# Down projection of two chunks as one Strassen pair, with a denser hand-out of attention steps: a fused attention and feed-forward block on one core

## The chip, the cores and the metric

The kernel runs on 1 core of one Trainium2 chip. The metric is device time in microseconds (us). All times compared here are of runs in the fast state; the two single runs e17 and e18 have no state, and only their traces are used. Medians are quoted beside ratios. A ratio is the mean time of one kernel's fast runs over that of the kernel before in the same rounds, so it is not quite the ratio of the medians.

Engines are named as the profile names them: PE is TensorE, PEld its weight loads, DVE VectorE, ACT ScalarE, POOL GpSimd.

## The reference

One pre-norm block over 2048 positions of width 1024, in bf16. Attention has 32 heads of 32; each position looks at 8 positions, at distances 0, 2, ... 14. The feed-forward part is the product of two linear maps, of width 3584.

```python
def _A_ref(x, wqkv, wo):               # H = 32, Dh = 32, W, dil = 8, 2
    q, k, v = ...                      # from x @ wqkv
    idx = pos[:, None] - arange(W)[None, :] * dil
    logits = einsum("bhsd,bhswd->bhsw", q, kg) * Dh ** -0.5   # kg, vg: k, v gathered by idx
    logits = where(idx >= 0, logits, -1e9)
    o = einsum("bhsw,bhswd->bhsd", softmax(logits), vg)
    return o.reshape(B, S, D) @ wo
def _B_ref(x, w_gate, w_up, w_down):
    return ((x @ w_gate) * (x @ w_up)) @ w_down
h = x + _A_ref(_layernorm(x), A_wqkv, A_wo)
return h + _B_ref(_layernorm(h), B_w_gate, B_w_up, B_w_down)
```

## The kernel before

The positions are cut into four chunks of 512. Chunks 0 and 1 go through the feed-forward part one after the other; chunks 2 and 3 go together, as a Strassen pair (7 block products where 8 would be needed). Attention is done on VectorE in steps that the program counts as 1.0 to 3.5 us (their instructions take 0.3 to 2.3 us each in the trace), and these steps are handed out between TensorE's groups of eight matmuls by a small scheduler. It runs when the program is built, so it fixes the order of each engine's queue and nothing else:

```python
class Background:
    def step(self, us):                       # called after each group of matmuls
        self.now += us
        self.credit = min(self.credit + us * self.rate, 4.0)      # the cap
        while self.credit > 0:
            item = next((i for i in self.items if i[0] <= self.now), None)
            ...                               # next attention step; credit -= its length
    def spend(self, us):                      # other VectorE work
        self.credit -= us
```

Chunk 0's output projection is followed by two blocks of the last QKV projection:

```python
    qkv(3, range(4), last=True)
    bg.finish(atts[0])
    bg.rate = 0.98
    nxt = wo_ln2(0)          # output projection; add, statistics, normalize on VectorE
    qkv(3, range(4, 6), last=True)
    start_attention(3)
    hT = ffn1(0, lnT2)       # first feed-forward of chunk 0: gate, up, product
    bg.finish(atts[1])
    nxt = wo_ln2(1)
    for hf in range(2):
        ffn2(0, hf, hT, hs)  # direct down projection of chunk 0
    ...
    hT = ffn1(1, lnT2, {...})
    ...                      # chunk 1's down projection as a small Strassen product of its own
```

The products run in float16 and need a power-of-two scale. It comes from the sum of absolute values: ScalarE adds up each tile, VectorE adds up the columns, a matmul with ones adds up the partitions, and five small VectorE steps make the scale. With several tiles ahead of it, such a scale is a chain through three engines:

```python
class Scale:
    def add(self, k, src, junk):
        nc.scalar.activation(junk, src, ACTF.Abs, accum_out=self.l1[:, k:k + 1])
    def rows(self):
        nc.vector.tensor_reduce(row[:], self.l1[:], ..., ALU.add)
        nc.vector.tensor_copy(self.rowb[:], row[:])
    def total(self, ps=None):
        nc.tensor.matmul(ps[:, 0:n], lhsT=ones[:], rhs=self.rowb[:]..., start=True, stop=True)
        ...                                   # five small steps on VectorE
```

## Time and profile before

| | kernel before |
|---|---|
| median of the first 3 runs, span | 776.96 us (776.87 to 777.28), 775.2 us |
| TensorE matmuls (weight loads counted) | 3691, 769.3 us busy, granted clock 1.00 in all records |
| VectorE, ScalarE busy | 605.3 us, 484.0 us |

The lines of the profile stand in the prediction. A line of busy times gives the share of the span behind each engine. A line of waits reads "engine, tile and line that waited <- what released it: us in total, times, longest". A line of the timeline gives start, length, engine, line, operation, and in brackets the idle time of that engine just before it. A line of a stretch gives its length, then the busy time of PE, PEld, DVE, ACT and POOL, then the granted TensorE clock, the busy share of the DMA engines and GB/s.

### The profile page before, as it was taken

The page shows a single profiled execution, that of the slowest core. Times are in us where ns is not written, and L with a number is a line of the kernel's source. Part 1 is how long each engine was busy: PE and PEld are TensorE (multiplying, and loading weights), DVE is VectorE, ACT ScalarE, POOL GpSimd, SP SyncE. Part 2 cuts the span into 40 slices and gives each one's busy share as a digit, 9 for nine tenths or more (in the row PEclk, how much of TensorE's full clock was granted, in tenths as well). Part 3 has the DMA queues.
Part 4 walks back from the last instruction along what each step waited for, and adds up shares of the span by engine and source line. Part 5 has one row for each costly group of instructions (what it writes and reads, how often), then busy time and mean ns, then how long its engine had stood idle before and what let it go on. Part 6 is the DMA issues. An engine that isn't in the chain of part 4 may idle for free.

```text
span 775.2 us, 10420 instructions
## 1 busy us (share of the span) xinstructions
PE 769.3 (99%) x3691; PEld 353.5 (46%) x3691; DVE 605.3 (78%) x766; ACT 484.0 (62%) x1040; POOL 142.1 (18%) x152
## 2 busy tenths in 40 slices
PE   8999999999999999999999999999999999999998
PEld 6444444444444444444444444444444444444444
DVE  5639999999999989999979859985553444578863
ACT  4639564322866662965777899746677776788240
POOL 0000000200002000011000001008778687600000
PEclk9999999999999999999999999999999999999999
DMA  8998896997947964978445592644332423740001
GB/s 278 265 260 199 157 230 151 299 271 224 310 133 236 308 235 125 288 257 277 142 143 192 182 299 68 157 98 114 109 95 69 109 59 106 240 140 28 0 28 55
DMA packets 183716, 134.38 MB, mean 173 GB/s; under 512 B 81264, under 2 KB 176496, under 8 KB 181616
## 3 DMA queue, kind: packets, MB, share of 16 engines
q1 hardware_dynamic: 176912, 110.12, 50.9%
q0 software_dynamic: 3584, 22.02, 8.9%
q10 hardware_dynamic: 3168, 1.57, 0.8%
q8 instruction: 29, 0.48, 0.3%
q14 instruction: 23, 0.19, 0.1%
HBM read 104.86 MB, written 22.02 MB: 164 GB/s over the span
## 4 chain that ended last, share of the span: by engine, by line
PE 93%; DVE 3%; DMA 2%; ACT 1%; issue 0%; ACTq 0%; DVEq 0%
PE ps L411 20%; PE pg L411 12%; PE pu L411 12%; PE dx L807 6%; PE pz L700 6%; PE acc L646 6%; PE py L700 6%; PE px L700 6%; PE wo L532 4%; PE wo L852 4%; PE pv L700 3%; PE dy L807 3%; PE ex L807 2%; DMA lnT<-lnr 1%; DMA w_qkv<-in_A_wqkv_dram 1%; PE ps L372 1%
## 5 line engine op out<-in xcount | busy, mean ns | idle before, releaser
L411 PE MATMUL ps<-lnT,w_qkv 128*128 128x512 bf16 x736 | 159.5, 379 | 0.0
L411 PEld LDWEIGHTS <-w_qkv 128*128 128x128 bf16 x736 | 71.9, 98 | 86.2
L411 PE MATMUL pu<-lnT,w_wu 128*128 128x512 bf16 x448 | 105.8, 379 | 0.0
L411 PE MATMUL pg<-lnT,w_wg 128*128 128x512 bf16 x448 | 105.8, 379 | 0.0
L324 ACT CAST sg<-ps 128x512 bf16<-128x512 f32 x96 | 55.2, 585 | 52.3 <-PE ps L411 49.2
L451 DVE TENSOR_TENSOR prod<-qD,kD 128x4096 bf16<-128x4096 bf16 x32 | 72.4, 2285 | 12.8 <-DMA kD<-kd 12.7
L494 DVE TENSOR_TENSOR pv<-vD,at 128x4096 bf16<-128x4096 bf16 x32 | 72.5, 2285 | 0.3
L700 PEld LDWEIGHTS <-sw 128*128 128x128 f16 x448 | 43.8, 98 | 53.8 <-issue 1.2
L411 PEld LDWEIGHTS <-w_wu 128*128 128x128 bf16 x448 | 43.8, 98 | 52.9
L411 PEld LDWEIGHTS <-w_wg 128*128 128x128 bf16 x448 | 43.7, 98 | 52.8
L616 ACT CAST us<-pu 128x512 bf16<-128x512 f32 x56 | 33.0, 590 | 43.0 <-PE pu L411 41.8
L700 PE MATMUL px<-lnT,ws 128*128 128x512 bf16 x224 | 55.2, 379 | 0.0
L700 PEld LDWEIGHTS <-ws 128*128 128x128 f16 x336 | 32.9, 98 | 39.7
L506 POOL DMA_DIRECT2D od<-oD x4 | 2.2, 542 | 264.3 <-DVE oD L504 264.3
L646 PE MATMUL acc<-w_wd,gs 128*128 128x512 bf16 x224 | 48.5, 379 | 0.0
L681 POOL TENSOR_TENSOR sw<-ws 128x512 f16<-128x512 f16 x26 | 30.0, 1152 | 85.1 <-PE py L700 77.8
L611 ACT CAST gs<-pg 128x512 bf16<-128x512 f32 x56 | 32.6, 583 | 12.9 <-PE pg L411 10.6
L453 DVE TENSOR_TENSOR prod<-prod 128x4096 bf16<-128x4096 bf16 x16 | 36.6, 2289 | 0.4
L560 ACT ACTIVATE junkd<-w_wd 128x512 bf16<-128x512 bf16 x56 | 34.3, 613 | 0.0
L646 PEld LDWEIGHTS <-gs 128*128 128x128 bf16 x224 | 21.9, 98 | 26.4
L617 DVE TENSOR_TENSOR gs<-gs,us 128x512 bf16<-128x512 bf16 x56 | 23.5, 419 | 12.5 <-ACT us L616 12.5
L185 ACT ACTIVATE rs<-mv,eps 128x1 f32<-128x1 f32 (+1 forms) x21 | 6.2, 297 | 42.0 <-DVE mv L182 36.6
(321 smaller groups left out, 1391.5 us busy)
## 6 DMA issues: line engine op xcount, KB each, us to landing
w_wg<-in_B_w_gate_dram SPq DMA_DIRECT2D x14, 1024.0 KB, 6.7
w_wu<-in_B_w_up_dram SPq DMA_DIRECT2D x14, 1024.0 KB, 5.4
w_wd<-in_B_w_down_dram SPq DMA_DIRECT2D x8, 896.0 KB, 6.2
w_pair<-in_B_w_gate_dram SPq DMA_DIRECT2D x14, 512.0 KB, 4.0
w_pair<-in_B_w_up_dram SPq DMA_DIRECT2D x14, 512.0 KB, 5.2
w_wo<-in_A_wo_dram SPq DMA_DIRECT2D x6, 1024.0 KB, 6.2
w_qkv<-in_A_wqkv_dram SPq DMA_DIRECT2D x5, 1024.0 KB, 11.0
kd<-sg SPq DMA_DIRECT2D x32, 144.0 KB, 3.3
```

The source lines that it names most:

```text
L324: nc.scalar.copy(sg[:, HB:HB + TC], ps[:])
L411: nc.tensor.matmul(ps[:], lhsT=wt[:, ko, bass.ts(j, 128)], rhs=rhs[:, ko, :], start=(ko == 0), stop=(ko == KO - 1))
L451: nc.vector.tensor_tensor(prod[:, j], qD[:], kD[:, :, o:o + SUB], ALU.mult)
L453: nc.vector.tensor_tensor(prod[:, :, 0:16], prod[:, :, 0:16], prod[:, :, 16:32], ALU.add)
L494: nc.vector.tensor_tensor(pv[:, j], vD[:, :, o:o + SUB], at[:, w, None, :].to_broadcast((128, DH, SUB)), ALU.mult)
L532: nc.tensor.matmul(ps[:], lhsT=oTs[c][:, kk, t, :], rhs=wts["wo", c, hf][:, kk, :], start=(kk == 0), stop=(kk == KO - 1))
L560: nc.scalar.activation(junk, src, ACTF.Abs, accum_out=self.l1[:, k:k + 1])
L611: nc.scalar.copy(gs[:], pg[:])
L616: nc.scalar.copy(us[:], pu[:])
L646: nc.tensor.matmul(acc[t][:], lhsT=hT[f][:, bass.ts(t, 128)], rhs=wts["wd", c, hf, b][:, j, :], start=(f == 0), stop=(f == NF - 1))
L700: nc.tensor.matmul(ps[:], lhsT=lhs[:, ko, :], rhs=rhs[:, ko, :], start=(fresh and ko == 0), stop=(ko == 3), skip_group_check=not fresh)
L807: nc.tensor.matmul(ps[:, bass.ds(lo, n)], lhsT=lhs[k][:, bass.ts(q, 128)], rhs=rhs[k][:, bass.ds(lo, n)], start=(fresh and k == 0), stop=( ...
```

## The change

The intent is to save matmuls. Both chunks' down projections become one Strassen pair: 392 matmuls in place of 224 direct ones and 196 of the small Strassen product. For that, both first feed-forwards come first; chunk 1's products go out to HBM and are read back; and the attention has to be done earlier against the matmuls. So it is handed out 7% denser (a rate of 1.05 in place of 0.98), with twice the credit (a cap of 8.0 in place of 4.0). To make room on VectorE, the norm of chunk 1 and some conversions and copies ("seeds") go to ScalarE.

```diff
-        self.credit = min(self.credit + us * self.rate, 4.0)
+        self.credit = min(self.credit + us * self.rate, 8.0)
...
-    bg.rate = 0.98
+    bg.rate = 1.05
+    bg.spend(5.0)
     nxt = wo_ln2(0)
     qkv(3, range(4, 6), last=True)
     start_attention(3)
-    hT = ffn1(0, lnT2)
-    bg.finish(atts[1])
-    nxt = wo_ln2(1)
-    for hf in range(2):
-        ffn2(0, hf, hT, hs)
+    def wo_1():
+        bg.finish(sums)
+        bg.finish(atts[1])
+        n = wo_norm(1)                 # output projection of chunk 1, its norm on ScalarE
+        ...
+    hT0 = ffn1_first(nxt[0], {4: wo_1})
+    bg.finish(norm2[1])
+    ffn1_second(norm2[0].lnT, {})      # products to HBM from a ring of three tiles
...
+    while 3 not in scored:
+        next(atts[3])
+    wo_adds(2, {0: in_turn(lambda: pull(1), lambda: abs_blocks(b11 + b21)), 2: in_turn(scale_h1.rows, lambda: pull(1)),
+                4: in_turn(total_h1, lambda: pull(1)), 6: lambda: pull(1)})
+    for q in range(4):
+        dprod(xs[q], q, A11, cells_of(b11, NH), True)       # first of seven products
+        if q == 0:
+            conv_h1(a21, 0)            # conversions of what is read back from HBM
+            conv_h1(a22, 0)
+            s1_half(0)
+            scale_d.rows()             # column sums of the down weights' scale
+        if q == 1:
+            pull(1)                    # one attention step
+            conv_h1(a21, 1, nc.scalar)
+            conv_h1(a22, 1, nc.scalar)
+        if q == 2:
+            scale_d.total(ys[3])
+            ...
+            for i in range(3):
+                seed(i)
...                                    # six more products, results, order of loads
```

## The prediction

> **What bounds the kernel now.** I read the page's first lines, then TensorE's own waits, then the chain of waits, then busy time by stage, and last the stretches of VectorE, ScalarE and GpSimd that feed the stages which the change rearranges.

> From the page (1: busy time; 2: the span in 40 slices; 4: the chain that ended last):

> ```profile
> span 775.2 us, 10420 instructions
> PE 769.3 (99%) x3691; PEld 353.5 (46%) x3691; DVE 605.3 (78%) x766; ACT 484.0 (62%) x1040; POOL 142.1 (18%) x152
> ...
> PE   8999999999999999999999999999999999999998
> DVE  5639999999999989999979859985553444578863
> ...
> PE 93%; DVE 3%; DMA 2%; ACT 1%; issue 0%; ACTq 0%; DVEq 0%
> ```

> TensorE (PE) is busy 99% and carries 93% of the last chain. Busy matmul time by itself would not prove a limit, so I checked the spacing in the chain of waits in order of time:

> ```profile
> 287.88 13.81 PE wo L532 x64
> 301.69 48.35 PE acc L646 x224
> ...
> 446.76 6.04 PE ex L807 x28
> ```

> 64, 224 and 28 matmuls of 512 columns take 13.81, 48.35 and 6.04 us: 0.216 us each, with no gap between these stages. All of TensorE's waits in the run:

> ```profile
> PE warm_ps L318 <- DVE warm L304: 1.2, 1, 1.2
> PE pv L700 <- DVE h L812: 0.6, 2, 0.4
> PE ps L372 <- ACT lnT L367: 0.4, 1, 0.4
> PE ps L372 <- DMA w_qkv<-in_A_wqkv_dram: 0.3, 1, 0.3
> PE pt L366 <- DVE ln L359: 0.3, 1, 0.3
> ```

> These 2.8 us and the tail are all the idle time there is. So each matmul taken away is worth 0.216 us, there is nothing left to hide a new wait behind, and a new wait costs its whole length. VectorE (DVE) is the second engine: the stages from 191 to 447 us, as columns PE, weight loads, DVE, ACT, POOL busy, show it at 95%, 98% and 90%:

> ```profile
> 191.00:302.00 111.00, 111.00 (x516) 50.31 (x515) 105.53 (x106) 66.31 (x126) 5.70 (x8) 1.00 0.75 236
> 302.00:350.00 48.00, 48.00 (x224) 21.77 (x223) 46.85 (x33) 35.30 (x116) 3.12 (x4) 1.00 0.78 243
> 350.00:447.00 97.00, 97.00 (x452) 43.94 (x450) 87.12 (x88) 73.69 (x161) 2.06 (x4) 1.00 0.57 185
> ```

> [...]4096 bf16 columns take 2285 ns as tensor-tensor and 1276 ns as tensor-scalar, so the new sums cost nearly twice a conversion of that size.[...]

> **The change part by part.**
> TensorE. Removed: the direct down projection of chunk 0 (4 row blocks x 2 halves x 28 = 224 matmuls) and the Strassen product inside chunk 1 (7 products x 2 blocks x 14 = 196). Added: one Strassen pair over both chunks, 7 x 4 x 14 = 392. Net 28 fewer, 28 x 0.216 = **6.04 us**. Two of the matmuls that add up a scale grow from 64 to 512 columns, 2 x 0.19 = 0.37 us back. The instruction order agrees (28 fewer matmuls in all). Gain if nothing waits: **5.67 us**, 771.3 us.

> VectorE. The number of instructions falls from 766 to 718, but they are larger (4096-wide sums of chunk 1's activations, 512-wide in place of 256-wide sums); summing counts by the durations in the trace, the totals are equal within 1 us. What changes is the deadline. TensorE used to reach chunk 2's output projection at 452.8 us; now it comes after both first feed-forward stages: 191.2 + 193.4 + 13.8 = 398.4 us. Chunk 1's output projection moves from 287.9 to 191.2 + 32 x 1.727 = 246.4 us. The 1.05 rate and the larger credit are there to have attention 1, 2 and most of 3 done by then.

> ScalarE. It loses abs sums of 512 columns (613 ns plus 187 ns for the read of the sum) and gets 2048-wide ones; it gains sums of the down weights after the fact (12 of 1024 and 4 of 512 columns, about 12 x 1.05 + 4 x 0.6 = 15 us), seeds, and half of the conversions. By the row durations it stays under 80% in both feed-forward stages, but at the down stage its queue becomes a chain.

> Transfers. Chunk 1's products go to HBM and return (3.7 MB out, 5.5 MB back), against some 3.7 MB less of down weights. At a mean DMA share of 0.6 in that stretch these stay hidden.

> **Where TensorE may wait: the near meets.** I add VectorE's durations in the new order, from its first attention product at 52.0 us. The same addition on the old order gives 233.3 us for the start of attention 1's last sum, once the 2.8 us of waits seen in its trace are added; the trace has 233.6, so the method holds within 0.5 us.
> 1. Output projection of chunk 1 (due 246.4). Attention 1 ends near 235.3. Before, these GpSimd steps lay so:

> ```profile
> 236.17 0.54 POOL L506 DMA_DIRECT2D od<-oD  x1 [62.50 <-DVE oD L504]
> 245.09 3.54 POOL L509 DMA_DIRECT2D oT<-od  x4 [8.39 <-PE pg L411]
> ```

> The store took 8.9 us, and the first of four loads 3.7 us more: with the same weights in flight, 235.3 + 8.9 + 3.7 = 247.9. Wait about 1.5 us.
> 2. Scale of chunk 1's products, a matmul behind five groups of chunk 2's output projection (398.4 + 1.5 + 8.6 = 408.5). It needs the last product, its abs sum on ScalarE and two VectorE steps: about 409.4. Wait about 1.
> 3. Scale of the down weights, behind three blocks of the first product (near 424). ScalarE's 15 us of sums start near 407, and VectorE's own queue gets there near 424.4. Wait about 1.
> 4. The second product overwrites the banks that ScalarE must first copy into seeds: two 3072-wide conversions (2.7 us each by the 3267 ns of a 3584-wide one) stand ahead of the copies, so 422 + 5.4 + 0.7 = 428.1 to 428.8 against TensorE's 428. Wait about 0.7.
> 5. In the stage of chunk 3's output projection VectorE has near 26 us of adds, statistics, conversions and sums for 25.9 us of matmuls (13.8 + 12.1); the first result must leave its bank before the next product. Wait about 1.3.

> The sum is 5.5 us, nearly all of the gain: 776.8 us. But each is the difference of two estimated arrivals: it may come out at zero, a wait in one absorbs part of the next, and the constants (1.05, which steps sit on ScalarE) look as if they had been fitted on the chip against just these waits. I choose some 3 us in all: 776.96 - 5.67 + 3.0 = **774.3 us**.

> **The rivals.**
> A. No wait: the scheduling is exact and the whole 5.67 us comes out, 771.3 us. For it: the kernel before has no gap either, in a schedule as tight. Against it: five meets within 2 us.
> B. VectorE becomes the bound of the middle. If its queue is 4 us later than I add up (longer waits for exp, products waiting for ScalarE), meets 2 to 4 move with it: 5.67 lost and some more, 777 to 780 us. For it: 95 to 98% busy before, and 54 us less until its deadline.
> C. The round trip through HBM or the late weight loads arrive late: the reads wait for the last store, then bring 3.5 MB, some 10 to 14 us at 250 to 350 GB/s, due near 417. Against it: the order puts three 512-wide adds and three attention steps ahead of the conversion. If late by 3 us, 776 to 778 us.

> **Range and chances.** Best case 771.3 less a little noise, so 770.8 below; my full sum of waits plus 2 us for B or C, 778.8 above. Faster by over 2% would need 15.5 us; only 5.67 are there. Slower by over 2% would need 21 us of waits, over three times the sum.

> **What would show it.** TensorE's busy time near 763.6 and 3663 matmuls. Attention 1's store issued near 235 and chunk 1's output projection near 246 to 248. In TensorE's waits, a few rows of 0.5 to 2 us: output projection on a transfer, scale matmuls on VectorE, second product on ScalarE's seeds. Wrong if these rows sum to over 7 us or to nothing, if TensorE waits in the pair stage after, which I take as unchanged, or if the stages before 163 us move.

## The result, and the profile after

The changed kernel is correct and takes **784.90 us** (median of 4 runs, 783.94 to 785.59); the kernel before took 777.04 us in the same rounds. The ratio is 1.010, interval 1.0083 to 1.0118. So it is 1% slower, not 0.3% faster, and lies 6.1 us above the predicted range.

The page of the changed kernel (span, busy times, chain that ended last):

```profile
span 782.0 us, 10253 instructions
...
PE 764.8 (98%) x3607; PEld 351.9 (45%) x3663; DVE 606.4 (78%) x718; ACT 511.9 (65%) x979; POOL 142.0 (18%) x152
...
PE 65%; DVE 21%; ACT 5%; issue 4%; DMA 4%; SPq 0%; DVEq 0%; ACTq 0%
```

The matmuls did go: 3663 weight loads against 3691 are 28 fewer. (The trace misses some matmul records, so the loads are counted.) But TensorE carries only 65% of the last chain, where it carried 93%; VectorE now carries 21%. TensorE's waits after 60 us, in the changed kernel:

```profile
PE l1psh L641 <- DVE rowbh L636: 3.6, 1, 3.6
PE pwu L430 <- ACT ring L756: 2.0, 1, 2.0
PE pg L430 <- DMA lnT<-ln: 2.0, 1, 2.0
PE ey L641 <- DVE rowbd L636: 1.4, 1, 1.4
...
PE ps L430 <- DVE h L600: 0.4, 1, 0.4
PE ex L931 <- ACT ey L1054: 0.2, 1, 0.2
```

They sum to 9.6 us. Three stretches of the changed kernel tell more:

```profile
191.20:199.00 7.80, 5.78 (x20) 2.17 (x19) 6.37 (x11) 4.78 (x15) 0.00 (x0) 0.78 0.99 276
275.00:300.00 25.00, 24.89 (x116) 11.31 (x116) 18.48 (x23) 24.84 (x47) 1.07 (x2) 1.00 0.71 210
416.90:423.70 6.80, 6.65 (x25) 2.80 (x26) 6.70 (x11) 6.80 (x15) 0.00 (x0) 0.79 1.09 355
```

In the first and the third, each right at a wait, the granted clock is 0.78 and 0.79. That is 7.8 x 0.22 + 6.8 x 0.21 = 3.1 us lost on top of the waits, an estimate from these two lines. In the second ScalarE is busy 24.84 of 25 us while VectorE, which should be the full engine, has 18.48.

The sum of the span: 5.67 us saved, 9.6 us of waits, 3.1 us of slow clock, and 0.6 us of waits of the kernel before near 520 us that are gone: +6.4 us. The spans differ by 782.0 - 775.2 = 6.8 us. So the gain is there, and more than twice as much is lost in four places:

1. **At 191 us**, where the first feed-forward starts, it waits for the last transposes of chunk 0's norm. VectorE's first addition of chunk 0's output projection, in the timeline of the kernel before and then of the changed one:

```profile
171.99 0.69 DVE L534 TENSOR_TENSOR h<-wo,h 128x512 bf16<-128x512 f32 x1
```

```profile
176.82 0.68 DVE L600 TENSOR_TENSOR h<-wo,h 128x512 bf16<-128x512 f32 x1
```

It starts 4.8 us later, because three more attention steps (2.29, 1.22 and 1.23 us) stand ahead of it in the queue.

2. **At 384 us** TensorE waits for a bank that ScalarE has not yet copied. ScalarE's timeline there:

```profile
383.03 1.06 ACT L631 ACTIVATE ring<-ring 128x1024 bf16<-128x1024 bf16 x1 [4.31 <-DVE ring L739]
```

ScalarE stood 4.31 us before an abs sum, for a product that VectorE had behind some 9 us of attention 3, and the copies that TensorE needed stood behind that sum and an exp of 1.04 us. In the trace the next copies come only at 385.03 us, after both.

3. **At 413 us**, the scale of chunk 1's products (3.6 us). 4. **At 434 us**, the scale of the down weights (1.4 us).

### The profile page after: what moved, and what is told of

Same layout as the page of the kernel before. It is cut to its first block, busy times and chain, and to the rows that moved or that the text cites.

```text
span 782.0 us, 10253 instructions
## 1 busy us (share of the span) xinstructions
PE 764.8 (98%) x3607; PEld 351.9 (45%) x3663; DVE 606.4 (78%) x718; ACT 511.9 (65%) x979; POOL 142.0 (18%) x152
## 3 DMA queue, kind: packets, MB, share of 16 engines
q0 software_dynamic: 3584, 22.02, 8.6%
q10 hardware_dynamic: 6864, 5.24, 2.5%
HBM read 110.10 MB, written 27.26 MB: 176 GB/s over the span
## 4 chain that ended last, share of the span: by engine, by line
PE 65%; DVE 21%; ACT 5%; issue 4%; DMA 4%; SPq 0%; DVEq 0%; ACTq 0%
PE ps L430 18%; PE dx L931 6%; PE pz L813 6%; PE py L813 6%; PE px L813 6%; DVE pv L521 5%; DVE prod L476 4%; PE pv L813 3%; PE ez L931 3%; PE ey L931 3%; PE dy L931 3%; DVE oD L531 2%; PE wo L985 2%; DMA w_wg<-in_B_w_gate_dram 2%; DMA a<-hd 2%
## 5 line engine op out<-in xcount | busy, mean ns | idle before, releaser
L476 DVE TENSOR_TENSOR prod<-qD,kD 128x4096 bf16<-128x4096 bf16 x32 | 72.0, 2285 | 12.9 <-DMA kD<-kd 12.8
L430 PE MATMUL pg<-lnT,w_wg 128*128 128x512 bf16 x221 | 53.4, 383 | 2.2 <-DMA lnT<-ln 2.0
L430 PE MATMUL pwu<-lnT,w_wu 128*128 128x512 bf16 x219 | 52.5, 379 | 2.3 <-ACT ring L756 2.0
L813 PE MATMUL px<-lnT,ws 128*128 128x512 bf16 x212 | 53.1, 379 | 0.6
L430 PE MATMUL pu<-lnT,w_wu 128*128 128x512 bf16 x218 | 53.3, 384 | 0.3
L430 PE MATMUL pwg<-lnT,w_wg 128*128 128x512 bf16 x220 | 52.5, 379 | 0.2
L931 PEld LDWEIGHTS <-gs 128*128 128x128 f16 (+1 forms) x280 | 27.4, 98 | 34.9 <-issue 2.1
L830 ACT COPY py<-px 128x512 f32<-128x512 f32 x28 | 16.0, 570 | 28.2 <-PE px L813 28.2
L631 ACT ACTIVATE ring<-ring 128x1024 bf16<-128x1024 bf16 x14 | 14.8, 1059 | 25.8 <-DVE ring L739 25.8
L795 POOL TENSOR_TENSOR sw<-sw,ws 128x512 f16<-128x512 f16 x26 | 30.0, 1154 | 2.0
L797 POOL TENSOR_TENSOR sw<-ws,sw 128x512 f16<-128x512 f16 x26 | 30.2, 1161 | 0.0
## 6 DMA issues: line engine op xcount, KB each, us to landing
w_qkv<-in_A_wqkv_dram SPq DMA_DIRECT2D x5, 1024.0 KB, 10.8
```

Source lines behind the costliest of these rows:

```text
L430: nc.tensor.matmul(ps[:], lhsT=wt[:, ko, bass.ts(j, 128)], rhs=rhs[:, ko, :], start=(ko == 0), stop=(ko == KO - 1))
L476: nc.vector.tensor_tensor(prod[:, j], qD[:], kD[:, :, o:o + SUB], ALU.mult)
L795: eng.tensor_tensor(sw[:, i, 1], sw[:, i, 0], a11, ALU.subtract)
L797: eng.tensor_tensor(sw[:, i, 3], a12, sw[:, i, 1], ALU.subtract)
L813: nc.tensor.matmul(ps[:], lhsT=lhs[:, ko, :], rhs=rhs[:, ko, :], start=(fresh and ko == 0), stop=(ko == 3), skip_group_check=not fresh)
L830: nc.scalar.copy(yb[i][:], xb[i][:])
```

## The experiments

Two theories were set against each other. **Q**: each wait stands for itself and comes from one step in a wrong place of a queue; mend the place and the time is won. **V**: VectorE (with ScalarE, which it feeds and waits for) sets the pace of the whole middle, and a wait taken away comes back at the next place where TensorE meets it. Further rivals were the read-back through HBM and the transfers (C), and the density of 1.05.

| run | what it is | median us | ratio to before | TensorE's larger waits, us |
|---|---|---|---|---|
| changed | | 784.90 | 1.0100 | 2.0, 2.0, 3.6, 1.4 |
| e1 | cap of 4.0 up to chunk 0's projection | 780.09 | 1.0045 | 2.5, 3.6 |
| e2 | kernel before, cap of 8.0 | 781.96 | 1.0060 | 2.3, 1.4 |
| e3 | cap of 4.0 throughout | 780.18 | 1.0039 | 2.0, 3.6 |
| e4 | changed, six gate sums left out | 779.51 | 1.0035 | 1.8, 3.1, 1.0 |
| e5 | e1, scale matmul later | 782.85 | 1.0070 | 1.7, 5.9 |
| e6 | e5, two more steps moved | 788.04 | 1.0153 | 2.4, 1.4, 4.9, 4.0 |
| e7 | e6, chunk 1's projection later | 787.52 | 1.0133 | 1.7, 2.3, 4.9, 4.1 |
| e8 | changed, rate 0.98 | 785.32 | 1.0103 | 1.9, 8.7 |
| e9 | e1, two norms to ScalarE | 780.82 | 1.0050 | 2.0, 2.6, 1.1 |
| e10 | e1, two gate sums moved | 776.69 | 0.9998 | 2.8, 2.3 |
| e11 | e9 and e10 | 777.30 | 1.0006 | 1.7, 2.5 |
| e12 | e11, rate 0.98 | 785.85 | 1.0117 | 1.7, 11.1 |
| e13 | e10, down scale earlier | **775.12** | **0.9980** | 2.6, 0.7, 1.1 |
| e14 | e10, chunk 1's projection later | 777.55 | 1.0005 | 4.3, 0.8 |
| e15 | e13 and e14 | 777.56 | 1.0010 | 3.8, 0.9, 1.1 |
| e16 | changed, two gate sums moved | 780.71 | 1.0047 | 0.6, 2.0, 3.1, 2.5 |

Intervals of the ratios reach 0.0012 to 0.0015 to either side (0.0018 for the changed kernel). The runs were taken in several rounds, on different chips; the changed kernel was run in the first alone, and the medians of the kernel before were 777.02 to 777.25 us in all of them. The waits are those of the one profiled run of each kernel, which need not be a typical one: e1's is its slowest (781.86 of 779.46 to 781.86 us), e5's its fastest (780.29 of 780.29 to 784.39). All of them give the correct result, e4 too, whose scale is wrong on purpose.

### e1 to e3: the cap

```diff
-        self.credit = min(self.credit + us * self.rate, 8.0)
+        self.credit = min(self.credit + us * self.rate, self.cap)    # 4.0; e1 sets 8.0 after start_attention(3)
```

> The changed kernel with the old cap of 4.0 until chunk 0's output projection has been built, and 8.0 after it: three attention steps (2.29 + 1.22 + 1.23 us) no longer stand ahead of that projection's first addition on VectorE. Both theories: the 2.0 us wait of TensorE at the start of the first feed-forward and the slow clock after it (2 x 0.8 us) are gone, TensorE enters that stage near 191.3 instead of 193.55. Theory Q (each wait stands for itself, a matter of queue order): the 3.7 us stay won to the end, 781.2 us. Theory V (VectorE is now the engine that sets the pace of the middle, and the waits of TensorE only show where the two meet): TensorE, now 3.7 us early, finds chunk 1's attention output not landed at 246.8 (it landed near 249.5) and waits 2 to 3 us there, and the waits at 383, 413 and 434 us keep their places: at most 1.5 us of the 3.7 remain, 783 to 785 us.

> The kernel before with the cap raised from 4.0 to 8.0 and nothing else. If the cap is what puts the attention steps ahead of chunk 0's output projection, TensorE waits 2 to 3 us at the first matmul of the first feed-forward near 191 us (its last normalize moves from 187.0 to about 190.4) and runs the next two groups slowly, so the time rises by 3 to 4 us to about 780.5. If the rate of 1.05 or the handing of steps after chunk 0's projection is the cause instead, nothing changes: 777 us.

> The changed kernel with the old cap of 4.0 throughout. The wait at 191 us goes as in the run before it. Theory Q: the burst of nine us of attention steps ahead of a product of chunk 1 at 373 to 382 us is cut in two as well, so the 2.0 us wait at 383 us goes too: 5.7 us less, 779 us. Theory V: with a lower cap steps that could not be handed out are lost rather than saved, so VectorE has less in its queue and falls further behind at 400 us: the waits at 413 and 434 us grow by what the first two gave, 784 to 787 us.

e2 settles the first place: the cap alone makes the kernel before 4.9 us slower (776.77 to 777.43 against 780.56 to 782.59), with the wait at 194.96 us (2.28 us) and a clock of 0.72 in the 6 us after it:

```profile
PE pg L411 <- DMA lnT<-ln: 2.3, 1, 2.3
```

So the larger credit, not the density, puts the three steps ahead. In e1 that wait is gone and 4.8 us are won, more than the 3.7 expected; not all of it is the price of this one wait, as those at 384 and 434 us are gone too. Still both theories missed something. TensorE's waits in e1:

```profile
PE l1psh L642 <- DVE rowbh L637: 3.6, 1, 3.6
PE wo L575 <- DMA oT<-od: 2.5, 1, 2.5
```

As V says, TensorE, now on time, waits 2.5 us for chunk 1's attention output. In the changed kernel that wait was zero only because TensorE came 4 us late. Against V, the waits at 384 and 434 us are gone. e3 is the same as e1, so what the cap does after chunk 0's projection makes no difference to the time.

### e4: ScalarE's load

```diff
-                if j % 2:
+                if j % 2 and b < 4:
                     abs_sum("wg", b, j // 2, junk[:])
```

> The changed kernel without the last six of fourteen abs sums of the gate weights (ScalarE, 2048 columns, 1.92 + 0.21 us each; those columns of the sum are set to zero, so the scale may come out too large on purpose). It frees 12.8 us of ScalarE between 247 and 300 us. If VectorE is late because it waits for ScalarE there (5.0 us for the up casts, 1.1 for the exp in that stretch), VectorE gains 4 to 6 us by 300 us, the first addition of chunk 2's output projection moves from 412.6 to about 407, and the waits at 413 and 434 us shrink from 5.0 to 0 to 2 us: 780 to 782 us. If ScalarE's load is not the cause, the time stays at 784.9.

The time fell by 5.4 us, a little more than expected. VectorE's waits for the up copies fell from 5.0 to 1.1 us, and the first addition of chunk 2's projection moved from 412.6 to 408.3 us. Part of the gain is luck: in the run that was profiled, the wait at 191 us (1.81 us) was not followed by the slow clock. That ScalarE holds VectorE up between 270 and 300 us is shown.

### e5 to e7: moving the places where TensorE waits

```diff
-                4: in_turn(total_h1, lambda: pull(1)), 6: lambda: pull(1)})
+                4: lambda: pull(1), 6: lambda: pull(1), 7: total_h1})          # e5
             conv_h1(a21, 0) ...                                                # e6:
+            scale_d.rows()                     # ahead of the conversions
-            conv_h1(a21, 1, nc.scalar) ...     # both behind the seeds
-    hT0 = ffn1_first(nxt[0], {4: wo_1})
+    hT0 = ffn1_first(nxt[0], {(4, 2): wo_1})                                   # e7
```

> The kernel of e1 with the matmul that adds up the scale of chunk 1's products moved from behind five groups of chunk 2's output projection to behind all eight. TensorE reaches it 5.2 us later, so its wait of 3.65 us there is gone (both theories), and with it the slow stretch after it in the runs that have one. Theory Q: 3.7 to 5 us less than e1's 780.1, about 775.5 us. Theory V: the next meeting is kept by VectorE, which still adds up the down weights' sum near 432.0 us behind the read-back of chunk 1's products and three 4096-wide steps; TensorE, now at about 428.5, waits 3 to 4 us there instead, and the time stays near 779 to 780 us.

> The kernel of e5 with two steps moved in their queues: VectorE adds up the down weights' sums before it converts what is read back (ScalarE has the last of them at 426.6 us), and ScalarE copies the seeds before its two 3072-wide conversions of 2.84 us each. Nothing is removed from any engine. If the waits are a matter of where four small steps stand, TensorE has no wait after 402 us: 3 to 5 us less than e1, 775.5 to 777 us. If VectorE's total load or the read-back is the limit, a wait of the same size appears at the next product, the ones that use the read-back near 445 us, and the time stays at 779 to 780 us.

> The kernel of e6 with chunk 1's output projection called after two of the four column groups of gate block 4 instead of before them, 6.9 us later. TensorE meets chunk 1's attention output, which lands near 249.5, at 253.7: the wait of 2.5 us there is gone. Theory Q: that stays won, 772.5 to 774.5 us, under the kernel before. Theory V: VectorE and ScalarE pay for it with the later norm, the start of chunk 1's feed-forward waits for its transposes near 302 us, and no more than 1 us is won over e6.

The wait of 3.6 us is gone in e5, and the next one has grown from nothing to 5.9 us, with a slow clock after it:

```profile
PE ey L642 <- DVE rowbd L637: 5.9, 1, 5.9
PE wo L575 <- DMA oT<-od: 1.7, 1, 1.7
```

e5 lost 2.8 us against e1 by the medians, worse than either theory said. e6 lost 5.2 more, by its own edit. The seeds came 4.9 us late, since the small steps of the down weights' scale still stood in VectorE's queue behind the conversions and an attention step; ScalarE, which had been given nothing else to do first, was idle for 8.04 us. Then VectorE stood 7.89 us for the two ScalarE conversions that I had moved back, and the third product waited 4.0 us for VectorE. So e6 does not decide between load and order; it shows that moving one step without what it needs only moves the wait. In e7 the wait for the attention output is gone, as expected, and the total stays within 0.5 us of e6, as V expected, though not in the place that V named: no wait appears near 302 us; two of 0.8 and 0.9 us on ScalarE's copies appear at 387 and 395 us instead, and the one at 425 us grows from 1.4 to 2.3 us.

### e8: the density

```diff
-    bg.rate = 1.05
+    bg.rate = 0.98
```

> The changed kernel with the old rate of 0.98 in place of 1.05 for the attention steps after chunk 0's output projection has started; the cap stays 8.0. The wait at 191 us stays, as those steps are handed out before. If the density does what its author wanted, attention 1 ends some 2 to 3 us later and the output projection of chunk 1 waits for it, and more of attention 3 is left over at 397 us: same to 3 us slower, 785 to 788 us. If the density is what delays the products of chunk 1, the wait at 383 us goes and the time falls by 2 us, 783 us.

```profile
PE wo L985 <- DMA oT<-od: 8.7, 1, 8.7
PE pg L430 <- DMA lnT<-ln: 1.9, 1, 1.9
```

785.32 us, the same as the change. Three waits (2.0, 3.6 and 1.4 us) became one of 8.7 us at chunk 3's output projection, because attention 3 ended that much later (its last addition starts at 470.4 us, in the changed kernel at 460.6). The density does what its author wanted; it only chooses where the wait lies.

### e9 to e12: relief for VectorE, relief for ScalarE

e9 makes the norm of two of chunk 0's row blocks on ScalarE. e10 has the two abs sums of gate block 4 ahead of chunk 1's output projection, where ScalarE was idle 5.0 us:

```diff
-                if j % 2:
+                if j % 2 and b != 4:
                     abs_sum("wg", b, j // 2, junk[:])
...
+            if b == 4:
+                for i in range(2):
+                    abs_sum("wg", 4, i, junk[:])
             if b in at:
                 at[b]()                # wo_1
```

> The kernel of e1 with the normalization of two of chunk 0's four row blocks taken from VectorE (1.27 + 0.21 + 0.55 us each, 4.06 us in all) to ScalarE, which has 4.2 us of work in the 28 us of that stage. Theory V (VectorE's queue sets the time up to chunk 3's output projection): every step of VectorE after it comes 4 us earlier, attention 1 ends near 229.5, the 2.5 us wait of chunk 1's output projection is gone and the waits at 413 to 432 us shrink: 2.5 to 4 us less than e1, 776 to 777.5 us. Theory Q (single steps in wrong places): the wait for the attention output goes, the scale's wait of 3.65 us stays because it keeps its place in the queue, 777.5 us at best and the wait at 413 us unchanged. Theory C (transfers): the output of attention 1 lands when it did, 780 us.

> The kernel of e1 with the two abs sums of gate block 4's weights (4.2 us of ScalarE) done ahead of chunk 1's output projection, where ScalarE stands idle for 5.0 us, instead of among the casts after it. The same sums, the same result. If ScalarE's full queue from 270 to 300 us holds VectorE up there (4.6 us for the up casts in e1), VectorE gains 2 to 4 us by 300 us; by theory V that comes out as 1 to 3 us in the time, 777 to 779 us. If VectorE would wait elsewhere anyway, no change: 780 us.

> Both reliefs of the two runs before it. Theory V: they add up, since both are time of VectorE before the same deadline: 774 to 776 us, under the kernel before. Theory Q: the 3.65 us wait of the scale stays, 776 to 777.5 us.

> Both reliefs, with the old rate of 0.98 besides. With the rate of 0.98 alone the waits at 383, 413 and 434 us vanished and came back as one of 8.7 us at chunk 3's output projection, near 484 us, because attention 3 ended at 472.6. Theory V: the 4 us taken from VectorE and the 2 to 4 us that it no longer waits for ScalarE come off that one wait, the 3.6 us that TensorE is earlier add to it: 4 to 6 us of wait in that place and none before, 776 to 778 us. Theory Q: the one wait is a matter of that projection's place and stays at 8.7 or more, 780 to 782 us.

e9 failed as a test: VectorE was rid of 4.06 us, but then stood 5.60 us at 183.15 us for a root that ScalarE computed behind the moved norms. Attention 1's last addition came at 234.9 us, not earlier than e1's 233.2. The relief turned into a wait.

e10 is the most telling run. No work was removed, two sums were moved by a few us, and 3.4 us were won; the change is then level with the kernel before. VectorE's waits for the up copies in the changed kernel, in e1 and in e10:

```profile
DVE gs L696 <- ACT us L720: 5.0, 3, 2.8
```

```profile
DVE gs L697 <- ACT us L721: 4.6, 2, 3.2
```

```profile
DVE gs L697 <- ACT us L724: 0.7, 1, 0.7
```

They fell from 4.6 to 0.7 us, the column sums for the scale of chunk 1's products were ready at 411.3 us instead of 414.8, and the wait of 3.6 us there is gone. TensorE's waits that are left:

```profile
PE wo L575 <- DMA oT<-od: 2.8, 1, 2.8
PE ey L642 <- DVE rowbd L637: 2.3, 1, 2.3
```

But the length of the waits is the small part of what was won. After the first 50 us they sum to 6.2 us in e1 and 5.3 in e10, because the wait of 2.3 us at 428 us is new: a part came back, as V says. The large part is the clock. In e1 it was at half for 3.41 us behind the first wait and for 6.83 us around the second; in e10 it was at half once, for 3.41 us. Counted as half of what lies after each wait, that is 4.6 us lost in e1 and 1.7 in e10. The spans of the two profiled runs differ by 3.5 us. It is not one lucky run: the mean granted clock was 0.993 to 0.998 in the five runs of e1, 0.998 or 1.000 in the six of e10.

e11 adds nothing to it, as e9 gave nothing. e12 hurts V in its plain form: with the reliefs and the lower rate VectorE was not full at all. It stood 11.7 us before products of chunk 1, in one place 6.21 us, because no attention step had been handed out; and attention 3 was late by 11.1 us at chunk 3's projection. So there the order fixed when the program is built is the limit, and not VectorE's work. At the rate of 1.05 no run separates the two cleanly: in the changed kernel VectorE was busy 194.5 of the 206 us from 191 to 397 us, so a few us of waiting for ScalarE are enough to make it late. That these waits matter, e4 and e10 show.

### e13 to e16: what remains

```diff
             conv_h1(a21, 0)
+            scale_d.rows()
             conv_h1(a22, 0)
             s1_half(0)
-            scale_d.rows()
         if q == 1:
-            pull(1)
...
             inv1 = inv1[:]
+            pull(1)
             for i in range(3):          # e13; e14 is e10 with {(4, 2): wo_1}; e16 is the edit of e10 alone
```

> The kernel of e10 with the sum of the down weights' scale put between VectorE's two conversions (ScalarE has the last part at 423.2 us) instead of behind them and a 4096-wide addition, and with one attention step put behind the steps of that scale instead of before them. Local: the scale's matmul no longer waits (2.3 us), the seeds are copied near 429.8 to 432.2 and the second product waits some 0.6 us: 1.5 to 2 us less than e10, 774.7 to 775.2 us. Load: the wait returns at the seeds or at the third product near 442 us, as in e6: 776.7 us or more.

> The kernel of e10 with chunk 1's output projection, and the two sums ahead of it, called two column groups later in gate block 4 (6.9 us). Its attention output has then landed: the wait of 2.8 us is gone, and so is the slow stretch after it, 1.7 us in some runs. Local: 773 to 774 us. Load: VectorE and ScalarE get the norm of chunk 1 6.9 us later and the waits near 385, 412 or 428 us grow by 2 to 3 us: 776 to 777 us.

> Both moves of the two runs before it. Local: both waits gone, 771.5 to 773 us, the 5.67 us of removed matmuls nearly all out. Load: 776 to 777 us.

> The changed kernel with its cap of 8.0 and only the two abs sums of gate block 4 moved ahead of chunk 1's output projection. If the cap and ScalarE's full queue are independent causes, this gives the same 3.4 us that the move gave with the cap undone: 784.9 - 3.4 = 781.5 us, the wait at 191 us and its slow clock stay, those at 383 and 413 us go. If the move only helps once the first is gone, 784 to 785 us.

e13 came out where the theory of a local place put it, at 775.12 us. Its ratio is 0.9980, interval 0.9966 to 0.9994: under the kernel before, and 9.8 us under the change. Its waits:

```profile
PE wo L575 <- DMA oT<-od: 2.6, 1, 2.6
...
PE ev L936 <- DVE w_dn L929: 1.1, 2, 0.9
PE ex L936 <- ACT ey L1059: 0.7, 1, 0.7
```

In its profiled run the granted clock was 1.00 throughout. The arithmetic closes: 776.96 - 5.67 + 4.4 - 0.6 = 775.1 us. By its interval e13 is under the kernel before; that its edit is better than e10 is not shown. The runs of the two overlap (774.78 to 776.83 us against 775.22 to 779.18), the waits are only 0.9 us shorter in sum, and the wait of 2.6 us happened to be followed by no slow clock, where e10's of 2.8 us was.

e14 did not. The wait for the attention output is gone, TensorE reaches chunk 2's projection at 398.0 us, 5.2 us before e10, and then waits 4.35 us for the scale of chunk 1's products: its column sums are there at 411.1 us, against 411.3 in e10. VectorE waited 3.3 us for TensorE's projection in e10 and not in e14, but 2.9 us more for ScalarE between 285 and 300 us. From 190 to 420 us its waits sum to 10.8 us in e10 and 10.4 in e14, so its queue comes hardly earlier. That wait is not local. e15 shows the same, 3.8 us.

e16 completes a table of two by two: 784.9 with neither mended, 780.1 with the cap, 780.7 with the sums, 776.7 with both. The sums give 4.2 us alone and 3.4 us beside the cap; with runs that spread over 2 to 4 us, the table shows no dependence between the two causes. In e16 the wait at 384 us went, that at 413 us stayed at 3.1 us, which I had expected to go, and that at 434 us grew from 1.4 to 2.5 us: the waits sum to 8.2 us in place of 9.6, and one slow stretch in place of two makes up the rest of the 2.7 us by which the profiled runs differ.

### e17 and e18: the clock

In all traces up to here a slow clock, from the first feed-forward on, stood only at waits of TensorE or after its last matmul. To see whether the wait is the cause, six waits of chosen length were put into the first feed-forward of the kernel before (single runs, 824.70 and 826.76 us):

```diff
+    def stall(b, gs):
+        nc.gpsimd.tensor_copy(stall_a, gs[:, 0:1])
+        for _ in range((0, 2, 4, 6, 8, 12)[b - 1]):          # e18: the other way round
+            nc.gpsimd.tensor_copy(stall_b, stall_a)
+            nc.gpsimd.tensor_copy(stall_a, stall_b)
+        sp = psum.tile([128, TC], F32, tag="mm", name=f"stall{b}")
+        nc.tensor.matmul(sp[:, 0:64], lhsT=ones[:], rhs=stall_a.to_broadcast((128, 64)), start=True, stop=True)
```

> The kernel before with six waits of TensorE made on purpose in chunk 0's first feed-forward, one per gate block, each a matmul of 64 columns behind a chain of 1, 5, 9, 13, 17 and 25 copies of one column on GpSimd; the result is unchanged. Theory: the wait itself is what brings the slow clock. Then the groups of eight matmuls after the short ones take 1.73 us as always, and after those of some 2.5 us and more one or two groups take about 2.5 us, 1.1 to 2.7 us more per wait. Rival: the slow clock came from the work around (transfers at full share, the engines' load): then no group here is slow, as none is in the kernel before.

> The same six waits in falling order. If length decides, the long waits are again followed by slow groups, now in the first blocks; if it is an effect that builds up or belongs to a place, the slow groups stay in the later blocks.

Two of the six in e17, in TensorE's timeline (the second line of each is the group of eight matmuls after the wait):

```profile
214.10 0.21 PE L611 MATMUL stall<-halo,ones 128*128 128x64 bf16 x1 [3.17 <-POOL halo L606]
214.13 3.40 PE L411 MATMUL pu<-lnT,w_wu 128*128 128x512 bf16 x8
...
232.75 0.19 PE L611 MATMUL stall<-halo,ones 128*128 128x64 bf16 x1 [3.14 <-POOL halo L609]
232.78 1.89 PE L411 MATMUL pu<-lnT,w_wu 128*128 128x512 bf16 x8
```

In the trace of the changed kernel the granted clock was 0.50 in each of the two slow stretches at a wait, and each lasted 3.41 us (from 194.44 to 197.85 us and from 416.30 to 419.71). In e1 it was 0.81 over the 18 us from 412, which at half clock is twice 3.41 us. Half clock for 3.41 us is 1.7 us lost, an estimate from these stretches, and it lies within the 1.4 to 2.7 us seen.

## Why the prediction was wrong

**TensorE's saving: right.** 28 matmuls fewer; and e13 shows that the 5.67 us come out where waits stay small. Other signs that the prediction named came out too: TensorE was busy 764.8 us (763.6 predicted; the slow clock is in it), attention 1's store was issued at 235.74 us (235), TensorE did not wait in the pair stage after, and it reached chunk 0's output projection at 163 us as before. VectorE's total, said to be equal within 1 us, went from 605.3 to 606.4. The sum of the transfers was wrong: by the totals of the two profiles, HBM reads grew from 104.86 to 110.10 MB and writes from 22.02 to 27.26, 5.24 MB each, where the prediction has 5.5 - 3.7 and 3.7 MB; it left out the residual rows, which go out and back as well (1.57 MB by their tiles).

**The step that failed is the adding up of VectorE's durations "in the new order".** It was checked on the order of the kernel before only, with the waits seen in that trace added; for the new order there was no trace, and the addition has no time in which VectorE stands still for ScalarE. Up to attention 1 the sum held. Then, between 270 and 410 us, VectorE waited 5.0 us for the up copies, 3.4 for the exp and 2.7 for a ring tile. So the column sums of meet 2, put at "about 409.4", came at 417.0 us, and it cost 3.6 us instead of 1. Of these 7.6 us, the cap makes some 2.2 (e1 has the sums at 414.8) and the place of two gate sums 3.5 (411.3 in e10); the other 1.9 us are not traced. Behind it lies a second sentence: ScalarE "stays under 80% in both feed-forward stages". As a mean it held (82.4 of the 111 us from 191 to 302, 68.3 of the 95 us after), and it was of no use: in the 25 us from 275, where chunk 1's norm, the gate sums and the copies come together, ScalarE was 99% busy. e4 and e10 show this cause.

**A wait that was on no list: 191 us.** I took TensorE to arrive there at 191.2 as before and read the doubled cap as help for the deadlines. In fact the cap moves three steps ahead of a norm with almost nothing to spare: in the changed kernel TensorE could go on 3.9 us after the last normalize began; in the kernel before that one began at 187.0 us and TensorE came at 191.2. e1 and e2 show it, from both sides: 4.8 and 4.9 us, the slow clock and later waits included. The order of the two kernels' queues, which I had, showed these three steps.

**The five near meets**, with what they measured: chunk 1's attention output, 1.5 us predicted, 0 in the changed kernel (its 1 MiB store landed in 5.2 us there, with weights in flight, where the kernel before had 8.2 for this one and 4.6 to 8.2 for all four, and each 256 KB load took 6.9 to 8.6 us), but 2.0 to 2.8 us in e1, e3, e9, e10 and e13, where TensorE is on time; the step was right and hidden by the wait before it. The scale of chunk 1's products, 1 against 3.6. The down weights' scale, 1 against 1.4. The seeds, 0.7 against 0.2, and 0.7 in e13. Chunk 3's stage, 1.3 against 0. The wait at 384 us (2.0) was missing: I treated copies into TensorE's banks as free.

**The slow clock (3.1 us) was missing.** Waits were priced at their length; after a wait of 1.98 us or more the clock was slow in 31 of 40 cases, and it then cost some 1.3 to 2.9 us more after a single wait (half of the slow stretch that lay behind it).

**The choice of 3 us out of a sum of 5.5 was wrong in its reason.** I supposed that the constants had been fitted on the chip against just these waits. The runs give no sign of it: the density of 1.05 is worth nothing (e8), two sums on ScalarE stand in a place that costs 3.4 to 4.2 us (e10, e16), and the cap costs 4.8 us by itself. But the whole sum would have given 776.8 us, still 8 us short; the choice was the small part of the error.

**The rivals.** B, VectorE as the bound of the middle, came nearest in mechanism and was too small; it names products that wait for ScalarE, and e4 and e10 show such waits, but the runs do not separate them from VectorE's load. C, the late read-back, is seen as 2.0 us of VectorE's wait at 428 us, and e13 shows that it costs little once the scale no longer stands behind it (0.9 us of VectorE's time, none of TensorE's directly); no run took the round trip out, so its whole price stays unknown. A did not happen. The prediction named "wrong if these rows sum to over 7 us": they sum to 9.6.

What stays open: why VectorE waits 2.9 us more for ScalarE in e14, which keeps chunk 1's products at 411 us as in e10 though TensorE was 5 us earlier; what part of the gain of e10 would stay if the clock were never slow; and how the remaining 2.6 us for the attention output could be had without losing them again. Nor was it studied why some waits from 1.98 to 3.76 us were followed by the slow clock (15 of 24) and others not.

## What to carry to other kernels

When a list of durations predicts a queue, walk it with both engines at once and write down where one waits for the other; an engine's mean share over a stage hides the 25 us in which it is full (here ScalarE's 82.4 of 111 us, and 24.84 of the 25 us from 275). In a kernel where one engine is busy 99%, look first at what a change puts ahead of that engine's next input, and look at the granted clock behind each wait as well as at its length: here 31 of 40 waits of 1.98 us or more were followed by a slow clock, which cost an estimated 1.3 to 2.9 us more after a single wait. A small shift that makes a wait shorter can win more by the clock than by the wait (e10 against e1: 2.9 us by the clock, counted as half of what lies after each wait, and 0.9 by the waits). A wait that is not there may only be covered by an earlier one: mending the first shows it (chunk 1's attention output, 0 us in the changed kernel, 2.5 in e1).
